# A new order of tasks and loads for a spectral filter and an MLP that share one core

## The chip, the core and the metric

The kernel runs on one core of a Trainium2 chip. The core has five engines that work at the same time and wait for each other through semaphores: TensorE (PE in the profile) for matmuls, VectorE (DVE), ScalarE (ACT), GpSimd (POOL) and SyncE (SP), which here only issues DMA transfers. TensorE writes its results to PSUM, which has eight banks; VectorE and ScalarE move them from there to SBUF. The metric is the device time of one execution in microseconds.

## The reference

Two independent branches are computed and mixed by a gate.

```python
def _A_ref(x, w_r, w_i):                      # x: 1 x 2048 x 512
    X = rfft2(x.astype(float32))
    X = X * (w_r + 1j * w_i)                  # W: 2048 x 257
    return irfft2(X, s=(S, D)).astype(bfloat16)

def _B_ref(x, w1, b1, w2):                    # w1: 512 x 1792, w2: 1792 x 512
    h = einsum("bsd,df->bsf", x, w1) + b1
    act = h * tanh(softplus(h))               # mish
    return einsum("bsf,fd->bsd", act, w2)

g = sigmoid((x * gate_w).sum(-1, keepdims=True))
return g * _A_ref(...) + (1 - g) * _B_ref(...)
```

## The kernel before

The dense branch is made of large matmuls that wait for little. It works on four chunks c of 512 rows. For a chunk, `mm1_c_ft` (line 795) is the product with one of 14 column tiles of w1 and takes four matmuls of 128x512; ScalarE evicts it with `mish_c_ft` (L811). Then `mm2_t_part` (L830) is the product with w2 for the row tile t = 4c to 4c+3, in two halves of seven matmuls (for the last tile, t = 15, in three column pieces instead). `bev_t` scales its result by 1 - g on its way to SBUF (L776 on ScalarE, L777 on VectorE).

The spectral branch is a long chain of small steps. Both transforms are split so that their halves are matmuls with constant matrices:

1. x is loaded (`ld_x`). Tiles 0 to 7 are transposed on TensorE (`tr`, L481). Tiles 8 to 15 are transposed in 32x32 blocks on VectorE (`tp`, L489), and 16 transfers from SBUF to SBUF, the shuffles (`sh`, named `xT<-act` in the profile), put the blocks in place; eight of them are issued by SP, eight by GpSimd.
2. Sums and differences (`ts`, `td`), then the transform along D: `a1` (L533), evictions `eg` on ScalarE and `e1p`, `e1m` on VectorE into `Abuf`.
3. The first half of the transform along S: `s1_t` for t = 0, 2, ..., 14 (L559), evictions `e2_t` into `Ybuf`.
4. The first exchange: each `e2_t` is followed by two writes to DRAM, `r1wta` and `r1wtb` (`scr<-Ybuf`); when all 16 have landed, four reads `r1r0` to `r1r3` bring the data back with partitions and columns rearranged (`Abuf<-scr`).
5. The filter stage, for u = 0 to 7 in pairs v: `s2_u` (L656); two multiplies with the weights W on VectorE, `wmu0`, `wmu1` (L414, `Qb<-ps,WT`); two sums on GpSimd, `wzu0`, `wzu1` (L414, `Zb<-Qb`); side steps for the two real-valued frequencies (`cv`, `crv`, `rcc`, `cm`, `chs`, `wc`); and `s2i_v` (L716), evicted by `e4_v0`, `e4_v1`.
6. The second exchange: four writes `r2w`, then four reads `r2r` (again `scr<-Ybuf` and `Abuf<-scr`).
7. For each row tile t: `s1i_t` (L744), eviction `e5_t` (L409 or L410), `a1i_t` (L755), `gc_t` on ScalarE (L760, scaled by g), `sam_t`, `sap_t` on VectorE (L766), `sbm_t`, `sbp_t`, nearly all on GpSimd (L414, `Tg<-Qb`). `sum_t` on VectorE adds this to the dense part (L414, `xo<-xo,Tg`), and each second one is followed by the store of two tiles. For tiles 14 and 15 `fin_t` (L842) does dense scaling and adding in one.

The weights W come in 18 pieces: `ld_Wp`, `ld_Wm` (eight each, about 128 KB) and two small `ld_Wz`. The names end in the part (0 real, 1 imaginary) and the group (0 to 3). All of them must be there before the first multiply. Further loads on SP are `ld_w2_0`, `ld_w2_1` and the constants `ld_rf`, `ld_ri`. The gate needs 16 `gdot` on VectorE (L575) and one power on GpSimd (`gpow`).

The program builds the list of all 639 tasks with what each reads and writes. It doesn't decide their order: that is written out beforehand in the string `ORDER`. `schedule` reads it from left to right. An entry is a task number of two base-62 digits; where a task may run on several engines a letter follows that says on which; where it takes a PSUM tile a digit follows with its first bank. From the order and the banks `schedule` derives the waits: a task waits for what it reads, and a task that takes a bank waits for those that still evict from it. Each engine, SP as well, works through its own part of the list strictly in order, so a task that waits holds all behind it on its engine. At the front TensorE runs 18 matmuls on constants (`warm`, L430).

Of the kernel before, what the change touches and what calls it, by code (L numbers as in the profile page):

```python
# [165 lines left out]
class _Graph:  # L166
# [89 lines left out]
DIGITS = "0123456789ABCDEFGHIJKLMNOPQRSTUVWXYZabcdefghijklmnopqrstuvwxyz"  # L256
ENGINE = {"p": "pe", "a": "act", "v": "dve", "g": "pool", "s": "sp"}
ORDER = (
    "0M04005060P070208090A000B0Q0C010R0D0E0F0G0H0T0I0x60J0N0yv0K0z50L7510V0O7F211610v13312v7K47A714v767L0S7M770U787"
    "B0W7C1Zv7G1X0037H1av1l50X1b61n1m33J0Y1Y0Z1pv7D7P00a17518v1d1B791A7T67U15116v1C191E7R51c60b1F1G7I7Q1D7N1Q7f01N1"  # L260
    "vv7J7h11V7b21ov1ev1wv7O1U1S7V41W7g7c8307E7S8J21fv1J1M8977i1P8H534283332718K1O1T1L36841y20v1x01gv0g0j1K7W381z0i"
    "8L41I0l8D68701R8M7z4297x18820v2Bv1H2Av8A21v350c2Iv2Ca2Hv7X02Jv8E22a7d32fv2D60s807y0f7Y0p2iv2gv7e2Kv1h10o2L41qv"
    "8l02N1iv0k2M32Ea1k8B48510e2Pv0u2V22W60q8n70m2hv8C2F2Ov8m2X861j0h2Yv2Zv1r30n1sa2Qa8b02312k62j32G8F42av8I24v262t"
    "52l1u2u38o2b12v2mv2nv1t2xv8177v52ca2R125822d2wv2ya2z68G372oa2e8p32Sv7w2p4392qv3A7Z130a8t68r22U3C8N73E8Z47a318u"
    "8h52T3B8q8a2r8c3G8x33D3F2s320d8j13H3I0r3K3L0t8k3T7s68f48O3O7t3W3P03M3N3Q8s8i3U3X18g3R8Pa3hv3S3Y47j77p07ua3a7q3"
    "gv3lv8d63kv3jg8y3Z3b7k8e7rv3t23ig3u43ng43v3V3v4F07la7m63mg8z74H903w42v47v3x46v7n3c79P24Ov4G37oa44g3y63d9X50w45"
    "g49g3e9Q4I4Sv9Y8v23z8w4J8Q748g4Pv4Tv4K28R4L403f3o3p34b08Sv8T23rv4M419T74A3qa9U8U4B34N4d4Rg8Va3s4kv4Qg4lv4Da4c0"
    "4Vg4W9V74Ca4e4Ug4mg4pv4f9W4E8W24ov4ng4g44h4i9N34qg4X49F04j4Za9114Yv9O4rg4s4t4924uv4va4a9Z49D38X9459G9J64w9L79E"
    "9M9709a8Ya93a954x5915H35Aa5P751496v5Qa9b29K5R55S4y9c5v15f75n65Iv5J352v5U5K5B4985T5wa4z5325C5M5L5oa5D5Wg5Vg5E5x"
    "55Ng5gv5y605Og9R15z5p350545X699a9H45Ya6R75q5Fg566J65Gg5h09S6Ka556Sv62gA1v5r9d56B16T29e61g5s5i9A76x66L36U5k6Ca6"  # L270
    "V6D55ug5Z15j6309I6EA8v58g57g5a5tgA2v6M5mg6p46W9B9yv5lg6N6Yg6ya6qa6h26ia6O9f66z2A7v5c6G5b706Xg5dg64aA5v719i45eg"
    "650A36Z36Pg6F6r59l1669Ca6Ig6j79zv6s9g6Qg6aa6b39j9m729p267689s0AEv6k6HgA4v6Ag74v6u6c6t9v5A96l69g6mA06wvA6ABv6d9"
    "ka6eAAv6vv6ogAC9haADv6ng9nAHv6fg73g6ggAF9o9qAGv9rAI9t9w9u9x"
)
NBF = 14
SHQ = ("pool", "sp", "pool", "sp")
# [688 lines left out]
```

## Time and profile before

| | us |
|---|---|
| median of three runs | 131.43 |
| lowest and highest of them | 130.37 and 131.91 |
| profiled execution | 131.48 |
| span of the profiled execution, first to last instruction | 129.7 |

The trace covers the span; the 1.8 us between span and time lie around it. A row of the order of time gives start and length in us, the engine, the line and the operation, the tiles out<-in and how many instructions are merged; in brackets stands how long the engine was idle before and what ended that. A row of the chain of waits gives start, length and the engine, tile and line. A row of a table by stretches gives the stretch, its length, the busy time of the engine asked for with the number of its instructions, the granted TensorE clock, the DMA share and GB/s. The clock was 1.00 throughout.

### The profile page before, as it was taken

Reading aid. Unit: us, or ns where it says so; the run is one execution under the profiler, and the core shown is the slowest. Engines: PE = TensorE matmul, PEld = TensorE weight load, DVE = VectorE, ACT = ScalarE, POOL = GpSimd, SP = SyncE. Lnnn points to the kernel's source line nnn. Section 1 sums busy time; section 2 is a strip of 40 time slices with the busy share of each in tenths; the row PEclk is TensorE's granted clock in tenths of the full one; section 3 lists DMA queues with packets and bytes.
Section 4 is the critical chain, followed back from the end, with each engine's and each line's share of the span. In section 5 each row is a group of like instructions: output and inputs, shape, how many; then the busy total and the mean of one; then the engine's idle time right before and its main releaser. Section 6 shows DMA issues by size and latency. Waiting matters only on the chain.

```text
span 129.7 us, 2726 instructions
## 1 busy us (share of the span) xinstructions
PE 123.0 (95%) x1014; PEld 66.1 (51%) x1014; DVE 91.6 (71%) x178; ACT 69.4 (54%) x119; POOL 56.3 (43%) x90
## 2 busy tenths in 40 slices
PE   7999999999999999699999999999999999999960
PEld 5776546445554444344444444444447666555650
DVE  0456999898699981179499795541006997999992
ACT  1306777798997537500336047454077988674300
POOL 4000047000000009146879499930000799979770
PEclk9999999999999999999999999999999999999999
DMA  3999618799998667991000032555089000224045
GB/s 88 337 402 394 199 40 219 216 263 189 289 314 242 197 173 223 331 390 43 0 5 3 0 93 73 162 162 159 13 285 356 3 5 3 81 81 157 10 152 172
DMA packets 19293, 21.16 MB, mean 163 GB/s; under 512 B 1744, under 2 KB 15952, under 8 KB 19152
## 3 DMA queue, kind: packets, MB, share of 16 engines
q1 hardware_dynamic: 18176, 19.67, 48.6%
q10 hardware_dynamic: 816, 0.79, 1.9%
q0 software_dynamic: 288, 0.53, 1.5%
q8 instruction: 8, 0.13, 0.4%
q14 instruction: 5, 0.04, 0.1%
HBM read 13.64 MB, written 6.29 MB: 154 GB/s over the span
## 4 chain that ended last, share of the span: by engine, by line
PE 85%; DMA 5%; DVE 3%; POOL 2%; issue 1%; POOLq 1%; DVEq 0%
PE ps L795 37%; PE ps L830 29%; DMA Abuf<-scr 5%; PE ps L744 3%; PE ps L755 3%; PE ps L533 3%; PE ps L559 3%; PE ps L430 3%; POOL Tg L414 2%; PE ps L656 2%; PE ps L716 2%; DVE Qb L766 1%; PE ps L481 1%; DVE xo L842 1%; DVE xT L409 1%
## 5 line engine op out<-in xcount | busy, mean ns | idle before, releaser
L795 PE MATMUL ps<-xT,w_sb 128*128 128x512 bf16 (+1 forms) x240 | 53.8, 365 | 0.3 <-DVE xT L409 0.3
L830 PE MATMUL ps<-w_sb,act 128*128 128x512 bf16 (+2 forms) x252 | 52.2, 355 | 0.0
L811 ACT ACTIVATE act<-ps,b1f 128x512 bf16<-128x512 f32 x56 | 36.5, 687 | 26.6 <-PE ps L795 26.6
L830 PEld LDWEIGHTS ps<-w_sb,act 128*128 128x128 bf16 x252 | 22.8, 98 | 23.0 <-issue 0.6
L795 PEld LDWEIGHTS ps<-xT,w_sb 128*128 128x128 bf16 x240 | 22.3, 98 | 21.9 <-DVE xT L409 0.8
L414 POOL TENSOR_TENSOR Tg<-Qb 128x256 bf16<-128x256 f32 x29 | 22.6, 812 | 17.4 <-DVE Qb L766 17.4
L414 POOL TENSOR_TENSOR Zb<-Qb 128x510 bf16<-128x510 f32 x16 | 20.0, 1268 | 3.2 <-DVE Qb L414 2.6
L414 DVE TENSOR_TENSOR Qb<-ps,WT 128x1024 f32<-128x1024 f32 x16 | 18.9, 1215 | 3.4 <-PE ps L656 3.3
L766 DVE SCALAR_TENSOR_TENSOR Qb<-ps,gcol,Qb 128x256 f32<-128x256 f32 x32 | 13.6, 473 | 1.5 <-issue 0.8
L580 POOL TENSOR_TENSOR gcol<-omg,gdot 128x16 f32<-128x16 f32 x1 | 2.9, 2942 | 26.6 <-DVE Tg L575 26.6
L410 ACT ACTIVATE Ybuf<-ps 128x1024 bf16<-128x1024 f32 x9 | 9.1, 1024 | 6.5 <-PE ps L716 6.2
L414 DVE TENSOR_TENSOR Abuf<-ps,Tg 128x512 bf16<-128x512 f32 x16 | 10.4, 685 | 2.7 <-ACT Tg L540 1.5
L409 DVE CAST Ybuf<-ps 128x1024 bf16<-128x1024 f32 x7 | 8.6, 1223 | 3.8 <-PE ps L716 3.1
L379 POOL DMA_DIRECT2D xT<-act x8 | 4.0, 503 | 15.5 <-DVE act L489 15.5
L575 DVE SCALAR_TENSOR_TENSOR Tg<-xo,Tg 128x512 bf16<-128x512 bf16 x16 | 10.5, 685 | 0.2
L776 ACT ACTIVATE xo<-ps,omg 128x512 bf16<-128x512 f32 x11 | 7.3, 687 | 5.2 <-PE ps L830 3.5
L777 DVE TENSOR_SCALAR xo<-ps,omg 128x512 bf16<-128x512 f32 x3 | 2.3, 751 | 10.8 <-PE ps L830 10.8
L760 ACT ACTIVATE Qb<-ps,gcol 128x256 f32<-128x256 f32 x16 | 7.1, 473 | 4.3 <-PE ps L755 4.2
L414 DVE TENSOR_TENSOR xo<-xo,Tg 128x512 bf16<-128x512 bf16 x14 | 9.0, 653 | 0.0
L540 ACT ACTIVATE Tg<-ps 128x512 f32<-128x512 f32 x8 | 4.7, 594 | 6.2 <-PE ps L533 6.2
L410 ACT ACTIVATE Zb<-ps 128x512 bf16<-128x512 f32 x12 | 7.0, 603 | 1.0 <-PE ps L744 1.0
L409 DVE COPY xT<-ps 128x512 bf16<-128x512 bf16 (+1 forms) x6 | 2.9, 505 | 5.7 <-PE ps L481 5.7
(61 smaller groups left out, 88.1 us busy)
## 6 DMA issues: line engine op xcount, KB each, us to landing
Abuf<-scr SPq DMA_DIRECT2D x8, 512.0 KB, 6.8
scr<-Ybuf SPq DMA_DIRECT2D x16, 128.0 KB, 2.2
scr<-Ybuf SPq DMA_DIRECT2D x4, 512.0 KB, 2.9
w_sb<-in_B_w_dram SPq DMA_DIRECT2D x2, 896.0 KB, 6.6
out_dram<-xo SPq DMA_DIRECT2D x7, 256.0 KB, 2.0
xo<-in_A_x_dram SPq DMA_DIRECT2D x3, 512.0 KB, 7.5
rt<-c_rt SPq DMA_DIRECT2D x2, 512.0 KB, 7.4
WT<-in_A_w_r_dram SPq DMA_DIRECT2D x7, 128.5 KB, 5.6
```

Source lines behind the costliest of these rows:

```text
L379: t = G.add(name, queue, issue if issue != 0.62 or queue != "pool" else 1.0, lambda e: e.dma_start(dst, src), reads=reads, writes=writes, ...
L409: fs = {"dve": ("dve", dve_dur(n, rate=rate), lambda e: e.tensor_copy(out=dst(), in_=src())), "act": ("act", act_dur(n), lambda e: e.activ ...
L410: "act": ("act", act_dur(n), lambda e: e.activation(dst(), src(), AF.Copy))}
L414: f = lambda e: e.tensor_tensor(out=o(), in0=i0(), in1=i1(), op=op)
L540: G.add(f"eg_{t}", "act", act_dur(512), lambda e, gb=gb, pa=pas[0], pv=pv: e.activation(G0[:, gb].rearrange("p t c (m s) -> p t c m s", s= ...
L575: lambda e, t=t: e.scalar_tensor_tensor(out=junk[t % 2], in0=xo[:, t, :], scalar=1.0, in1=gwb, op0=ALU.mult, op1=ALU.mult, accum_out=gdot[ ...
L760: lambda e, t=t, sl=sl, p5=p5: e.activation(gC[:, sl, :].rearrange("p (i n) -> p i n", i=2), ps[:, p5.bank, :].rearrange("p (i n) -> p i n ...
L766: lambda e, t=t, sl=sl, p5=p5, o=o, op=op: e.scalar_tensor_tensor(out=st1[:, sl, o::2, :], in0=ps[:, p5.bank, :].rearrange("p (i n) -> p i ...
L776: G.add_multi(f"bev_{t}", [("act", act_dur(512, True), lambda e: e.activation(xo[:, t, :], ps[:, pd.bank, :], AF.Copy, scale=omg[:, t:t + ...
L795: ins = e.matmul(o if c < 2 else o.rearrange("p (a t j) -> p a t j", a=4, t=4), w1_sb[:, i, 128 * ft:128 * (ft + 1)], xTp[:, i, 512 * c + ...
L811: lambda e, c=c, ft=ft, pd=pd, hb=hb: e.activation(act[:, hb, ft, :].rearrange("p (t a j) -> p t a j", t=4, a=4), ps[:, pd.bank, :].rearra ...
L830: ins = e.matmul(ps[:, pd.bank, cs_], act[:, hb, ft, 128 * tl:128 * (tl + 1)], w2_sb[:, ft, cs_], start=(ft == 0), stop=(ft == NFT - 1))
```

## The change

Only the string `ORDER` changes; the first and last lines of the diff stand for its 20 lines, which are all new:

```diff
 ORDER = (
-    "0M04005060P070208090A000B0Q0C010R0D0E0F0G0H0T0I0x60J0N0yv0K0z50L7510V0O7F211610v13312v7K47A714v767L0S7M770U787"
+    "0M04000050N060107080P090A0B0C0U0D0E0F0G0H0O0I0Q0x40J0K0yv0z110v0L7A20S750113135027F67K77612v7G14v0R1av77037B0T"
...
-    "ka6eAAv6vv6ogAC9haADv6ng9nAHv6fg73g6ggAF9o9qAGv9rAI9t9w9u9x"
+    "a6ngADv6d71AHv6wg7274vA36fg6ggAEv73gAF9nAGv9q9oAI9r9t9u9w9x"
 )
```

The tasks, their code and what they depend on are the same. What differs, decoded with the task list:

**SP.** The first 12 issues are the same, up to `ld_Wp00`. Then, up to `r1r0`:

```
before: sh12 sh32 sh31 sh33 sh11 sh13 sh30 sh10 w2_1 Wm02 Wz0 Wm03 Wm10 Wm00 Wz1 Wp02 Wm12 Wp12 Wp10
        r1w0b Wm01 w2_0 Wp13 Wp11 r1w6a r1w0a Wp03 Wm11 r1w6b r1w4b r1w2b r1w2a r1w4a r1w10a r1w10b
        r1w8b r1w14a r1w8a r1w12a r1w12b r1w14b Wp01 Wm13 rf r1r0
after:  Wm00 Wp01 Wm01 sh12 sh31 sh11 sh13 sh30 sh33 sh10 sh32 Wm12 Wp11 Wm13 w2_0 Wm11 r1w2a Wp03
        r1w2b Wp13 Wz1 Wp12 r1w4b Wm02 r1w0a r1w0b w2_1 Wp02 r1w6b Wz0 Wm03 r1w6a r1w8a r1w8b r1w4a
        r1w10b r1w10a r1w12a r1w12b r1w14b r1w14a Wp10 Wm10 rf r1r0
```

From there to the last `r2r` nothing changes; the stores at the end have another order.

**TensorE.** The first matmuls keep their kinds and change places. `s1` runs in the order 2, 0, 4, 6, 8, 10, 12, 14 (before 6, 0, 2, 4, 10, 8, 14, 12). Around the filter stage (`2_13` stands for `mm1_2_13`, `M2_0` for a half of `mm2_2`):

```
before: rcw s2_0 s2_1 M0_0 M2_0 M2_1 2_2 M0_1 s2_2 s2_3 s2_4 M1_0 2_13 M1_1 rcc_0 3_6 s2_5 rcc_1 3_10 2_11
        M5_0 rcc_2 M5_1 s2i_0 s2_6 M6_0 3_8 M6_1 s2i_1 s2_7 3_9 M7_0 rcc_3 3_5 s2i_2 3_1 M8_0 s2i_3 M8_1 3_11
        3_0 M7_1 M9_0 3_3 3_4 M10_0 M9_1 s1i_1 s1i_2 s1i_3 s1i_0 3_12 a1i_3 ...
after:  rcw 2_3 M1_0 s2_0 s2_1 2_6 M4_0 M4_1 s2_2 s2_3 M1_1 M5_0 rcc_0 s2_4 s2_5 M6_0 M6_1 rcc_2 M5_1 rcc_1
        s2i_0 2_8 M3_0 s2_7 s2_6 2_4 2_7 M3_1 rcc_3 s2i_1 M9_0 M9_1 s2i_2 3_9 M7_0 s2i_3 3_8 3_10 M7_1 M11_0
        3_2 M8_0 3_6 3_5 M8_1 M10_0 s1i_1 s1i_0 s1i_3 s1i_2 M11_1 a1i_0 ...
```

Ahead of `s2_0` stand 39 `mm1` and 4 halves of `mm2` before, 38 and 5 after. The last on TensorE before: `a1i_14 mm2_14_0 a1i_13 mm2_12_1 a1i_12 mm2_13_1 mm2_14_1 mm2_15_0 mm2_15_1 mm2_15_2`. After: `a1i_14 mm2_12_0 mm2_14_0 a1i_15 mm2_12_1 mm2_14_1 mm2_15_0 mm2_15_1 mm2_15_2`.

**VectorE, ScalarE and GpSimd** follow the new order. Of the `e2`, those for t = 0, 4, 8, 12 stay on VectorE and the others on ScalarE. Behind the first `sa`, VectorE has three `e5`, one `bev` and two `sb` (before two, none and three); GpSimd has 30 `sb` (before 29). VectorE's last tasks:

```
before: sam_14 sap_14 sap_13 sam_13 sbp_14 sum_9 sap_12 sam_12 sum_8 sbm_14 sum_10 fin_14_1 sum_13 fin_15_0 sum_12
        fin_15_1 fin_15_2
after:  sam_14 sum_7 sap_14 sam_12 sbm_14 sum_10 sap_12 sap_15 sum_13 sam_15 sbp_15 sum_11 fin_14_1 sum_12 fin_15_0
        fin_15_1 fin_15_2
```

GpSimd's last tasks: before `sbp_13 sbm_13 sbm_12 sbm_15 sbp_12`, after `sbm_13 sbp_14 sbm_12 sbp_12 sbm_15`.

More of the change, by code (lines that the diff above doesn't have):

```diff
@@ L258 @@
 ORDER = (
-    "0M04005060P070208090A000B0Q0C010R0D0E0F0G0H0T0I0x60J0N0yv0K0z50L7510V0O7F211610v13312v7K47A714v767L0S7M770U787"
[L260 to L272, printed above, removed]
-    "ka6eAAv6vv6ogAC9haADv6ng9nAHv6fg73g6ggAF9o9qAGv9rAI9t9w9u9x"
+    "0M04000050N060107080P090A0B0C0U0D0E0F0G0H0O0I0Q0x40J0K0yv0z110v0L7A20S750113135027F67K77612v7G14v0R1av77037B0T"
@@ new lines @@
+    "787L0V1X47C1Zv7M0W1l37H7N1Y0X1m17P51n1547R37Q1751ov1pv7O1b17I16v7D1A1B1d0Y7V40Z7T718v1C8L18357S190a7U1c30b7J3J"
+    "1F7X61E1G7b78M7W8H11D7E1wv1I331vv1fv7Y1ev1qa8J42720c1Q0d0e1N791R348B61J1U1K1M1O1S8I357c1r01H848C28737291x31T1W"
+    "1ga1P1y57z68521z2Bv1sa7h321v1L1h02Av20v87722v1iv1V8K867d42Jv2Kv2hv2307i7Z32Hv2V22Iv802L57e0p24v7a7x40m2gv0r2Ca"
+    "7f60u2iv2X880n2N1t2W32D07g0h2M72fv7v22Zv2Ea1u2Pv0q0s0o2Ov2Qa2Yv367w8x52u67y262R00g8y2j72t22k31j2Sv1k8d42l2nv2v"
+    "0v0f2mv2G8r70j2aa2xv2wv8e2oa0i2F2b18s2ca2ya8F52p32qv388G8t08u2T2z6392U258z18j030a8953A7p42e8Z28b32d908D63B3D3C"
@@ new lines @@
+    "8A3F7j72r3E2s8v13G8c8k3I7k7q8153H32318a0k0l3K3O3P38f20t3L3M3Q7m03R823N8E3T7lv8g3X53Y23Z8w8l73S3hv8N13gv3W3kv3U"
+    "7ra3a3jg8O3t48m3ig3u63lv3b42v7n43v3w8Q23c33V3v7oa3mg4F43d3ng8Pa4G045g47v4H8T34I46v44g3x4J8U8Va3e4K60w8R4Ov3f4P"
+    "v3y749g8Sa4L3o3z3p38p748g3qa4Qg4Sv4Tv7s24c04e3ra8q4b34kv8h54Rg4d8i4Vg4M8n68o404N414A7t4f4lv4g74h4ov4B34Dv4W947"
+    "4Ug4i4ng4j954mg4pv3s4Ca96a4X34s4rg4Zv4Ya9V04qg8W14t34vv9T79W9X04E4a8X4ua9A39H49154w9P67ua9Y9N04x929729O59093v5"
+    "155Av9U9I5P75H45Qa52v8Yv9B9Cv5305B75R15Ia545C4y5f49J5565J35ga5D5v4985S9Q5K555wa58g5h05n64z5X45E5i5Gg505T6B75L5"
@@ L274 @@
+    "U5ov5Ya9R15Z65p46Ca9K5M9D799v5Fg5k9S5q57g5a5j6D35Ng6325Wg64a9b06J55Og5x19yv9E5c5b9d25y9Z66h79c5lg5Vg9zv9e6505s"
+    "9F25r6E5z6ia6R75dg9a9L46Kv5mg6p56G6F9G5egA1v666Z69MA06aa605ug6j35tg6L2A5v686x1A4v6M9i46b66Hg676Sa6T06Ig6k69g6q"
+    "a6c9j62g6OA7v9ka6r76N6U9f56yvA2v9l26z16m9g9m9p4ABv6Ag61g6s6l9s3AAv6Qg6Pg6V6og6WAC9v06uA8v6Yg6tA970A66e6vv6Xg9h"
+    "a6ngADv6d71AHv6wg7274vA36fg6ggAEv73gAF9nAGv9q9oAI9r9t9u9w9x"
 )
```

## The prediction

> **What bounds the kernel now.** I read the page's busy times first, then the chain of waits, then TensorE's order of time, then the queues of SP, GpSimd and VectorE at the places that the chain names.
>
> ```profile
> span 129.7 us, 2726 instructions
> PE 123.0 (95%) x1014; PEld 66.1 (51%) x1014; DVE 91.6 (71%) x178; ACT 69.4 (54%) x119; POOL 56.3 (43%) x90
> ```
>
> TensorE works 123.0 of 129.7 us. No task is added or removed, so that sum stays. Only three things can move: TensorE's idle time, what follows its last matmul, and how early the long transform gets through beside the dense work.
>
> ```profile
> 6.86 1.91 PE L795 MATMUL ps<-xT,w_sb 128*128 128x256 bf16 x16 [0.27 <-DVE xT L409]
> 55.31 0.63 PE L656 MATMUL ps<-Abuf,rt 64*32 64x256 bf16 x32 [1.23 <-DMA Abuf<-scr]
> 119.10 6.28 PE L830 MATMUL ps<-w_sb,act 128*128 128x512 bf16 x56
> ...
> 119.32 1.66 DVE Qb L766 x4
> 121.05 1.71 POOL Tg L414 x2
> 123.87 0.88 POOL Tg L414
> 124.95 0.72 DVE xo L842
> 126.75 0.52 DVE xo L842 x2
> ```
>
> The first three rows are TensorE's, in order of time; the bracket is the idle time before and what ended it. Its one large hole is 1.23 us, in front of the first filter matmul s2_0 (L656): it waits for the first exchange through DRAM (r1r0) to land. The last matmuls end at 119.10 + 6.28 = 125.38. The other rows are the end of the chain: it leaves TensorE at 119.3, goes through VectorE (the sa tasks, L766) and GpSimd (the sb tasks), and VectorE's last fin (L842) ends at 126.75 + 0.52 = 127.27, which is 1.9 after the last matmul. The remaining 129.7 - 127.27 = 2.4 us are the last store. So the end is set by VectorE and GpSimd, and those started late:
>
> ```profile
> 100.40:127.30 26.90, 25.89 (x55) 1.00 0.18 66
> 101.38 2.10 POOL L414 TENSOR_TENSOR Tg<-Qb 128x256 bf16<-128x256 f32 x3 [15.84 <-DVE Qb L766]
> ```
>
> The first row is VectorE alone from the first sa to the last fin: 25.89 busy of 26.90, 1.0 idle. GpSimd sat 15.84 us idle before its first sb. Whatever brings the first s1i (L744) forward moves this whole tail.
>
> **First exchange: SP's queue.** SP issues one transfer after the other, and each waits in that order.
>
> ```profile
> 7.26 0.58 SPq L379 DMA_DIRECT2D WT<-in_A_w_r_dram  x1
> 17.57 5.02 SPq L379 DMA_DIRECT2D xT<-act  x8
> 37.32 8.53 SPq L379 DMA_DIRECT2D scr<-Ybuf  x13
> 48.40 2.43 SPq L379 DMA_DIRECT2D Abuf<-scr  x4
> ...
> 48.40 6.87 DMA Abuf<-scr
> ...
> 26.56 2.43 DVE L414 TENSOR_TENSOR Tg<-xT 128x512 bf16<-128x512 bf16 x7
> ```
>
> After the first W piece (7.26) SP stands still until the last transpose lets the shuffles go (17.57). From there to r1r0 at 48.40 it issues 45 transfers almost without a pause, 8.53/13 = 0.656 us each. So r1r0 is late because SP is, not because its data are: the last s1 is over long before. The change puts three more W pieces into the dead time before 17.57, which leaves 42 issues: 3 x 0.656 = 2.0 us. r1r0 goes at 46.4 and, with the same 6.87 (the row of the chain), lands at 53.3. The three pieces can delay the shuffles behind them by what they still have to move; I take nothing. SP issued its last shuffle before 17.57 + 5.02 = 22.6, and VectorE reads shuffled data first at 26.56 (last row): what the 4 us leave after the landing is the cover, and each us beyond it would hold VectorE's evictions of the first stage. The early r1w2, r1w4 wait for their evictions in the same queue and would hold the W pieces behind them; TensorE now does s1_2 and s1_4 8 to 12 us earlier than before, so I cost that at nothing, with 1.4 us of cover (next paragraph).
>
> **TensorE up to s2_0.** The prices, from the chain (a dense up matmul group mm1, half a down group mm2, one s2i, four s1i):
>
> ```profile
> 60.58 0.86 PE ps L795 x4
> 61.45 1.51 PE ps L830 x7
> 86.13 0.57 PE ps L716 x32
> 97.82 0.89 PE ps L744 x16
> ```
>
> Counting the decoded queue, s2_0 has 38 mm1 and 5 half mm2 in front of it, before 39 and 4: +1.51 - 0.86 = +0.65. Its turn comes at 55.31 - 1.23 + 0.65 = 54.7. r1r0 lands at 53.3, so the hole goes, with 1.4 us to spare. If SP gained nothing the landing would be at 55.27 and the wait 0.6. The 0.27 at 6.86 stays: the tasks up to there have only changed places.
>
> **Filter stage and second exchange.** From s2_0 to the last s2i_3 the old queue took 86.13 - 55.31 = 30.8 us, with 9 mm1 and 12 half mm2 between; the new one has 5 and 12: 30.8 - 4 x 0.86 = 27.4, so s2i_3 comes at 82.1 instead of 86.1. From s2_0 to the first s1i there are 10 mm1 instead of 13 (17 halves in both): 97.65 - 55.31 - 2.6 = 39.7, so s1i_1's turn is at 94.4. The second exchange must fit:
>
> ```profile
> 93.08 1.76 SPq L379 DMA_DIRECT2D Abuf<-scr  x4
> DMA to landing us min/median/max: 4.0/5.4/6.7
> ```
>
> Before, its first read was issued at 93.08 and landed 4.0 later, 97.1, which is 11.0 after s2i_3. From 82.1 that is 93.1, 1.3 us ahead of s1i_1's turn. What is late next is GpSimd:
>
> ```profile
> 57.00:86.00 29.00, 22.77 (x32) 1.00 0.18 61
> 58.31 1.26 POOL L414 TENSOR_TENSOR Zb<-Qb 128x510 bf16<-128x510 f32 x1 [1.64 <-DVE Qb L414]
> 85.31 0.23 POOL L703 TENSOR_TENSOR Zb<-ch 128x8 bf16<-128x8 f32 x1
> L414 DVE TENSOR_TENSOR Qb<-ps,WT 128x1024 f32<-128x1024 f32 x16 | 18.9, 1215 | 3.4 <-PE ps L656 3.3
> 62.89 0.85 PE L656 MATMUL ps<-Abuf,rt 64*32 64x256 bf16 x48
> ```
>
> Its 32 filter tasks (wz and their small helpers) are 22.77 us of work, in order. Before they ran from 58.31 (3.0 after s2_0) to 85.54, so 4.5 idle. Now they start at 57.7, could end at 80.5, and s2i_3 wants them by 82.1: at most 1.6 us idle are allowed. I take it that this holds, because the idle time came from TensorE's order: the old queue gave the second pair, s2_2, at 62.89, 7.6 us after s2_0, and VectorE's 16 multiplies stood 3.3 us for such matmuls. The new one puts one mm1 and two halves between the pairs (0.86 + 3.02), so s2_2 comes at some 59.2, before the four multiplies of the first pair are over (54.7 + 0.5 + 4 x 18.9/16 = 59.9).
>
> **The tail.** s1i_1 at 94.4; then four s1i (0.89) and one half mm2 (1.51) and a1i_0 (0.22 and the drain of its last matmul) with its scaled eviction on ScalarE (0.47), some 1.0 together: the first sa starts at 97.8, before at 100.4. VectorE's list behind it is that of before with one more eviction and one more bev, and one sb less:
>
> ```profile
> L414 DVE TENSOR_TENSOR xo<-xo,Tg 128x512 bf16<-128x512 bf16 x14 | 9.0, 653 | 0.0
> L414 DVE TENSOR_TENSOR Tg<-Qb 128x256 bf16<-128x256 f32 x3 | 2.3, 765 | 0.0
> L409 DVE CAST Zb<-ps 128x512 bf16<-128x512 f32 x2 | 1.4, 686 | 0.1
> L760 ACT ACTIVATE Qb<-ps,gcol 128x256 f32<-128x256 f32 x16 | 7.1, 473 | 4.3 <-PE ps L755 4.2
> ...
> 99.57 0.22 PE ps L755 x4
> ...
> 97.86 0.75 DVE L777 TENSOR_SCALAR xo<-ps,omg 128x512 bf16<-128x512 f32 x1 [9.85 <-PE ps L830]
> ```
>
> 0.69 + 0.75 - 0.77 = +0.7, so 26.6 of work; with the old 1.0 idle the last fin ends at 97.8 + 26.6 + 1.0 = 125.4, and with 2.4 for the last store the span is 127.8. TensorE does not stand in the way: its last matmul is at 125.38 - 1.23 = 124.15. Nor does GpSimd: 30 sb of 22.6/29 = 0.78 from some 99 end at 122.4 to 123.5.
>
> ```profile
> L414 POOL TENSOR_TENSOR Tg<-Qb 128x256 bf16<-128x256 f32 x29 | 22.6, 812 | 17.4 <-DVE Qb L766 17.4
> ```
>
> The profiled execution took 131.48, 1.8 more than its span, and the median of the runs is 131.43, so both are one number here: 127.8 + 1.8 = **129.6**, 1.4% under before. Without idle time on VectorE the last matmul sets the end: 124.15, a fin of 0.5, the store 2.4, and 1.8: 128.8.
>
> **Rivals.** *The filter stage does not shrink.* If GpSimd idles its old 4.5 us there, s2i_3 waits until 57.7 + 22.77 + 4.5 = 85.0, 2.9 late, TensorE stands with nothing to put in (its queue is in order), and s1i and the tail go with it: 132.5. For it: GpSimd now has almost no slack, and each late multiply costs TensorE in full beyond 1.6 us. Against it: the pauses of before are named as waits for matmuls that now come sooner. Half of it gives 131.
>
> *Slower: the sums meet the adds.*
>
> ```profile
> 124.08 0.95 DVE L414 TENSOR_TENSOR xo<-xo,Tg 128x512 bf16<-128x512 bf16 x1
> 125.61 0.41 DVE L414 TENSOR_TENSOR xo<-xo,Tg 128x512 bf16<-128x512 bf16 x1
> 123.84 1.77 POOL L414 TENSOR_TENSOR Tg<-Qb 128x256 bf16<-128x256 f32 x2
> 101.00:126.00 25.00, 22.63 (x29) 1.00 0.15 56
> ```
>
> The same sum takes 0.95 beside GpSimd's last two adds (123.84 + 1.77 = 125.61) and 0.41 after them. The 14 have a mean of 0.65. If all 14 were long, VectorE would need 14 x 0.30 = 4.2 more, the end would go to 133.8; from 4 more long ones (2.2) the gain is gone, from 6 it is slower than before by 1%. For it: GpSimd now runs from 99 to 123 with hardly a pause, so most sums run beside it. Against it: before, GpSimd was busy 22.63 of 25.0 us while the sums ran (last row), hardly less, and their mean was 0.65. The Trainium skill has this as a rule (SBUF — State Buffer, Who interferes with whom): a VectorE instruction with both inputs in SBUF contends with a GpSimd one that reads SBUF, and the later one blocks until the other is done. By that rule the difference 0.95 - 0.41 is the rest of a GpSimd add, and the trace agrees, since an add is 0.81 and the loss 0.54. Read strictly, every sum that meets an add is long, which is this rival.
>
> *Bank turns.* The new queue often takes PSUM banks with little to spare: s2_4 reuses the banks of s2_2 when six multiplies are over, 54.7 + 0.5 + 6 x 18.9/16 = 62.3, and its turn (one mm1, four halves and some 1.1 of small matmuls after s2_0) is 62.7. Several such turns lost by 0.2 to 0.4 each give 1.5 to 2 us, 131.3. For it: their number; against it: the old queue, laid out as densely, lost nothing but the DMA wait.
>
> That the change does not do what it says (no earlier W) would need SP to be blocked at the pieces; they wait for nothing. Even then it costs the 0.6 above, 130.2.
>
> **Numbers.** A change of 1% (130.1 and 132.7) is about what a measurement of this kernel can tell from none: the three runs of before lie between 130.37 and 131.91. Chances: forecast 0.56, filter stage 0.20, sums 0.12, bank turns 0.12. Faster takes 0.52 of the forecast and 0.03 of the bank turns; same the rest of these, 0.12 of the filter stage and 0.04 of the sums; slower 0.08 and 0.08: 0.55, 0.29, 0.16. The range begins at 128.4, a little under the bound without idle time since each eviction on VectorE may overlap, and reaches to 132.4, which takes in the bank turns and nearly all of the filter case.
>
> **What would show it.** SP: three more W pieces before 17.6, r1r0 issued at 44 to 46.5. TensorE: s2_0 at about 54.8 with no DMA wait; s2i_3 near 82; first s1i near 94.5. GpSimd: idle under 1.6 us in the filter stage. VectorE: first sa near 98, last fin near 125.4, mean sum near 0.65. A TensorE wait on GpSimd (L716) shows the first rival, a mean sum over 0.8 the second, many short waits on banks the third. r1r0 landing after 55, or s1i waiting for its DMA, would prove the two exchange steps wrong.

## The result, and the profile after

| | before | after |
|---|---|---|
| median, us | 130.91 (4 runs) | 129.50 (4 runs) |
| lowest and highest, us | 130.37 and 131.91 | 129.17 and 129.98 |
| profiled execution, us | 131.48 | 129.98 |
| its span, us | 129.7 | 128.2 |

The measured ratio of the two is 0.988, with a 95% interval of 0.983 to 0.993: 1.2% faster (the two medians alone give 0.989). (The string `ORDER` has 15 lines, not 20 as the section on the change says.)

The order of time of the changed kernel, TensorE's rows at the places that the prediction named:

```profile
7.19 1.47 PE L795 MATMUL ps<-xT,w_sb 128*128 128x256 bf16 x12 [0.73 <-DMA w_sb<-in_B_w_dram]
...
55.28 0.63 PE L656 MATMUL ps<-Abuf,rt 64*32 64x256 bf16 x32
...
82.50 0.64 PE L716 MATMUL ps<-Zb,rt 32*64 32x256 bf16 x32
...
94.95 1.06 PE L744 MATMUL ps<-GMs,Abuf 128*128 128x128 bf16 x16
...
118.07 6.28 PE L830 MATMUL ps<-w_sb,act 128*128 128x512 bf16 x55
```

The row of s2_0 (55.28) has no bracket any more: the wait of 1.23 us for the first exchange is gone. s2i_3 comes at 82.50 (86.06 before), the first s1i at 94.95 (97.65). The last matmuls end at 118.07 + 6.28 = 124.35, 1.03 earlier than before, though 1.23 of waiting went: at 7.19 TensorE now waits 0.73 for a piece of w1, where it had waited 0.27 for VectorE.

SP in the same view:

```profile
7.43 2.58 SPq L379 DMA_DIRECT2D WT<-in_A_w_r_dram  x4
18.89 5.03 SPq L379 DMA_DIRECT2D xT<-act  x8
...
47.53 2.07 SPq L379 DMA_DIRECT2D Abuf<-scr  x4
```

Four pieces of W now stand in front of the shuffles. But the shuffles go out at 18.89, 1.3 later than before, and r1r0 at 47.53 instead of the 46.4 of the prediction.

The tail, by the end of the chain of waits (first fence), by the busy time of VectorE and then of GpSimd in stretches (second and third), and by groups of instructions (fourth; columns: busy time, mean ns of one, idle time before). A q behind an engine's name, as in DVEq and SPq, marks its sequencer, which waits and issues:

```profile
119.58 4.00 PE ps L830 x35
123.61 0.74 DVE xo L842
124.34 0.33 DVE xo L414
124.67 0.40 DVEq L900
125.07 0.52 DVE xo L842 x2
```

```profile
98.30:125.60 27.30, 26.04 (x57) 1.00 0.17 63
```

```profile
98.30:125.60 27.30, 23.31 (x30) 1.00 0.17 63
57.00:82.10 25.10, 22.67 (x32) 1.00 0.17 55
```

```profile
L414 POOL TENSOR_TENSOR Tg<-Qb 128x256 bf16<-128x256 f32 x30 | 23.3, 812 | 18.1 <-DVE Qb L766 18.1
L414 DVE TENSOR_TENSOR Qb<-ps,WT 128x1024 f32<-128x1024 f32 x16 | 18.8, 1213 | 0.1
L414 DVE TENSOR_TENSOR xo<-xo,Tg 128x512 bf16<-128x512 bf16 x14 | 8.8, 630 | 0.0
```

The last fin ends at 125.07 + 0.52 = 125.59, before at 127.27. The chain passes from TensorE to VectorE at 123.61, but that is not a wait for TensorE: the task there, fin_14_1, needs the matmuls of mm2_14_1, which were over at some 121.1, where the narrower ones of mm2_15 begin, and VectorE was busy with a sum until it began. The 14 sums have a mean of 0.630 (0.653 before). In the filter stage GpSimd's 22.67 of work lie between 58.27 (its first sum there) and 82.00, so it was idle 1.1 us, where it had been idle 4.5; and the multiplies wait 0.1 in all, where they had waited 3.4.

### The profile page after: what moved, and what is told of

It reads as the page before. It is cut to its first block, busy times and chain, and to the rows that moved or that the text cites. A ratio compares the mean times of both kernels' runs of the same rounds, so it can differ in the third digit from the quotient of the medians.

```text
span 128.2 us, 2717 instructions
## 1 busy us (share of the span) xinstructions
PE 121.6 (95%) x998; PEld 65.8 (51%) x1014; DVE 91.9 (72%) x178; ACT 67.1 (52%) x118; POOL 56.9 (44%) x91
## 4 chain that ended last, share of the span: by engine, by line
PE 80%; DMA 8%; DVE 4%; SPq 4%; issue 1%; DVEq 0%
PE ps L830 37%; PE ps L795 29%; DMA xo<-in_A_x_dram 8%; SPq L379 4%; PE ps L744 3%; PE ps L755 3%; PE ps L559 3%; PE ps L533 2%; PE ps L716 2%; DVE act L489 2%; PE ps L656 2%; DVE xo L842 1%; DVE Tg L414 1%; DVE Tg L575 0%; DVEq L900 0%
## 5 line engine op out<-in xcount | busy, mean ns | idle before, releaser
L830 PE MATMUL ps<-w_sb,act 128*128 128x512 bf16 (+2 forms) x240 | 50.3, 354 | 0.7 <-issue 0.2
L811 ACT ACTIVATE act<-ps,b1f 128x512 bf16<-128x512 f32 x56 | 36.0, 690 | 22.5 <-PE ps L795 17.2
L414 POOL TENSOR_TENSOR Tg<-Qb 128x256 bf16<-128x256 f32 x30 | 23.3, 812 | 18.1 <-DVE Qb L766 18.1
L776 ACT ACTIVATE xo<-ps,omg 128x512 bf16<-128x512 f32 x9 | 6.1, 688 | 13.7 <-PE ps L830 7.8
L414 DVE TENSOR_TENSOR Abuf<-ps,Tg 128x512 bf16<-128x512 f32 x16 | 10.1, 683 | 1.6 <-PE ps L533 1.6
L410 ACT ACTIVATE Ybuf<-ps 128x1024 bf16<-128x1024 f32 x9 | 9.1, 1022 | 2.9 <-PE ps L716 2.9
L777 DVE TENSOR_SCALAR xo<-ps,omg 128x512 bf16<-128x512 f32 x5 | 3.7, 747 | 9.5 <-PE ps L830 9.4
L410 ACT ACTIVATE Zb<-ps 128x512 bf16<-128x512 f32 x11 | 6.4, 603 | 1.8 <-PE ps L744 1.8
```

The source lines that it names most:

```text
L410: "act": ("act", act_dur(n), lambda e: e.activation(dst(), src(), AF.Copy))}
L414: f = lambda e: e.tensor_tensor(out=o(), in0=i0(), in1=i1(), op=op)
L776: G.add_multi(f"bev_{t}", [("act", act_dur(512, True), lambda e: e.activation(xo[:, t, :], ps[:, pd.bank, :], AF.Copy, scale=omg[:, t:t + ...
L811: lambda e, c=c, ft=ft, pd=pd, hb=hb: e.activation(act[:, hb, ft, :].rearrange("p (t a j) -> p t a j", t=4, a=4), ps[:, pd.bank, :].rearra ...
L830: ins = e.matmul(ps[:, pd.bank, cs_], act[:, hb, ft, 128 * tl:128 * (tl + 1)], w2_sb[:, ft, cs_], start=(ft == 0), stop=(ft == NFT - 1))
```

## The experiments

Each was timed against the kernel before on the same chip; ratios are to that, with a 95% interval. The key times of the profiled executions, in us from the start of the span:

| kernel | SP's first shuffle | r1r0 issued, landed | s2_0 | s2i_3 | first s1i | first sa | last matmul ends | last fin ends | span |
|---|---|---|---|---|---|---|---|---|---|
| before | 17.57 | 48.40, 55.27 | 55.31 | 86.06 | 97.65 | 100.42 | 125.38 | 127.27 | 129.7 |
| after, first profile | 18.89 | 47.53, 54.07 | 55.28 | 82.50 | 94.95 | 98.37 | 124.35 | 125.59 | 128.2 |
| after_again | 17.32 | 45.33, 52.07 | 54.50 | 81.72 | 94.17 | 97.59 | 123.57 | 124.81 | 127.4 |
| pieces_back | 17.47 | 48.12, 54.46 | 54.66 | 81.87 | 94.33 | 97.74 | 123.72 | 124.96 | 127.6 |
| pieces_after_x | 17.32 | 45.81, 52.72 | 54.55 | 81.77 | 94.22 | 97.64 | 123.62 | 124.85 | 127.5 |
| old_pieces_front | 17.80 | 46.98, 53.04 | 54.29 | 85.04 | 96.63 | 99.40 | 124.36 | 126.26 | 128.7 |
| a1i_late | 17.57 | 45.57, 51.77 | 54.95 | 82.17 | 94.62 | 99.55 | 125.02 | 126.27 | 128.9 |
| a1i_later | 17.68 | 46.01, 53.17 | 55.06 | 82.28 | 94.73 | 100.52 | 126.00 | 127.24 | 129.9 |
| e5_15_act | 17.91 | 46.34, 52.60 | 55.00 | 82.21 | 94.67 | 98.09 | 124.06 | 125.31 | 127.9 |

### Which part of the change brings the gain

**pieces_back**: the changed kernel, with the three early pieces put behind the shuffles again.

```diff
 SP:
-ld_Wp00 ld_Wm00 ld_Wp01 ld_Wm01 sh12 sh31 sh11 sh13 sh30 sh33 sh10 sh32 ld_Wm12
+ld_Wp00 sh12 sh31 sh11 sh13 sh30 sh33 sh10 sh32 ld_Wm00 ld_Wp01 ld_Wm01 ld_Wm12
```

> The changed kernel with its three added W pieces issued behind SP's shuffles again; all engines keep the new order. Theory (the gain comes from the new order on TensorE; the early pieces only keep the first exchange ahead of TensorE's turn): x12 lands near 15.0 instead of 16.35, the shuffles start near 17.6 instead of 18.9, the three issues come back behind them (2.0 us), so the first exchange read goes out near 48.2 instead of 47.5 and lands near 54.8; TensorE's turn for s2_0 stays near 55.2 and the time within 0.3 us of the changed kernel (129.5). Rival (the early pieces are the gain): the time goes back to that of the kernel before, 130.9, with a DMA wait of about 1 us in front of s2_0.

Measured: 129.70 us, ratio 0.987 (0.980 to 0.994). Its order of time, SP and TensorE:

```profile
48.12 2.08 SPq L379 DMA_DIRECT2D Abuf<-scr  x4
...
54.66 0.63 PE L656 MATMUL ps<-Abuf,rt 64*32 64x256 bf16 x32
```

r1r0 goes out as late as in the old kernel, lands at 54.46, and s2_0 starts at 54.66 without a wait. The early pieces buy margin (2.4 us in after_again, 0.2 here) and no measurable time in the new order. The margin of 0.2 is that of one execution: from issue to landing r1r0 took 5.9 to 7.2 us in the profiles of this study, here 6.34. By these it could land up to 0.7 behind s2_0's turn in other executions without the early pieces (an estimate). The gain is in the rest of `ORDER`.

**old_pieces_front**: the kernel before, with the same three pieces in front.

```diff
 SP:
-ld_Wp00 sh12 sh32 sh31 ...
+ld_Wp00 ld_Wm00 ld_Wp01 ld_Wm01 sh12 sh32 sh31 ...
```

> The kernel before with only the three W pieces moved in front of the shuffles. Theory: the first exchange read goes out some 0.7 to 0.9 us earlier than its 48.4 (2.0 us of issues saved, 1.3 lost because x12 lands later), the hole of 1.23 in front of s2_0 shrinks to about 0.4, and the time falls by some 0.8 at most, to 130.1 or above. Rival (the early pieces are the gain): the whole 1.4 us, 129.5.

Measured: 130.81 us, ratio 0.995 (0.991 to 0.999). Its order of time:

```profile
46.98 2.07 SPq L379 DMA_DIRECT2D Abuf<-scr  x4
...
54.29 0.63 PE L656 MATMUL ps<-Abuf,rt 64*32 64x256 bf16 x32
```

The hole in front of s2_0 goes here too, and everything behind it comes about 1.0 us earlier than before. So in the old order the pieces are worth 0.5%. In the new order no gain shows, since in pieces_back s2_0's turn came only when r1r0 had landed anyway.

**pieces_after_x**: the first profile had the shuffles 1.3 us late, because x12 (the last piece of x) had landed at 16.35 instead of 15.03. An interim theory held that the three pieces, in flight with x, had delayed it. Here the pieces wait on SP until x has landed.

```diff
-nbytes=256 * 514, bw=190e3, nd=16, issue=0.45)
+nbytes=256 * 514, bw=190e3, nd=16, issue=0.45, deps=[G.last_w[("x", 12)]] if (i, g) == (0, 1) else [])
```

(and the same for `ld_Wm00` and `ld_Wm01`)

> The changed kernel with its three early W pieces held on SP until x12 has landed; nothing else. Theory (the pieces in flight slow x12's landing): x12 lands near 15.0 again, the pieces still go out before the last transpose is over, the shuffles start near 17.6, the first exchange read goes out near 46.2 and lands near 52.8, over 2 us ahead of TensorE's turn; the time stays within 0.3 us, since nothing waits for that exchange. Rival 1 (x12's later landing is chance or comes from elsewhere): x12 stays at 16.3. Rival 2 (the end hangs on the first exchange): the time falls by about 1.3 us.

Measured: 129.29 us, ratio 0.983 (0.977 to 0.989).

**after_again**: the changed kernel once more, unchanged.

> The changed kernel once more, unchanged, for a second profile and a time beside the others of this set. Theory (the 16.35 us at which x12 landed in its first profile was chance, since two other kernels with the same pieces in flight had it at 14.3 and 14.9): x12 lands at 14.3 to 15.1, the first exchange read goes out near 45.6 and s2_0 starts near 54.6. Rival (the pieces in flight delay x12): x12 lands after 16 again. Time 129.3 to 129.7 in both.

Measured: 129.66 us, ratio 0.988 (0.984 to 0.991). SP in the order of time up to 20 us, pieces_after_x first and after_again second:

```profile
7.70 9.04 SPq L379 DMA_DIRECT2D WT<-in_A_w_r_dram  x4
17.32 3.10 SPq L379 DMA_DIRECT2D xT<-act  x5
```

```profile
7.53 2.58 SPq L379 DMA_DIRECT2D WT<-in_A_w_r_dram  x4
17.32 3.11 SPq L379 DMA_DIRECT2D xT<-act  x5
```

In the one the last piece is issued only after x is there (7.70 + 9.04 = 16.74), in the other all four by 10.1, and the shuffles go at 17.32 in both. x12 landed at 14.78 in both. So the interim theory fell: the pieces do not delay x, and the 16.35 of the first profile was that execution's own. It was also the slowest of its four runs (129.98; lowest 129.17). The ratio of pieces_after_x is lower than that of after_again, but the intervals overlap and none of its key times in the table is earlier, so no gain is claimed for it.

### What lateness costs behind the filter stage

**a1i_late** and **a1i_later**: dense work put back in front of the tail, so that the same tasks start it later. What ran as a1i_late moves only `mm2_10_1` (1.5 us), not both tasks that its expectation names; a1i_later moves both (1.51 + 0.86 = 2.4 us).

```diff
 TensorE, a1i_late:
-mm2_11_1 a1i_0 a1i_1 a1i_3 s1i_5 mm1_3_3 a1i_2 s1i_7 mm2_10_1
+mm2_11_1 mm2_10_1 a1i_0 a1i_1 a1i_3 s1i_5 mm1_3_3 a1i_2 s1i_7
 TensorE, a1i_later:
+mm2_11_1 mm2_10_1 mm1_3_3 a1i_0 a1i_1 a1i_3 s1i_5 a1i_2 s1i_7
```

> The changed kernel with 2.4 us of dense work (mm2_10_1 and mm1_3_3) moved from behind the first a1i tasks to in front of a1i_0; the sum of TensorE's work is the same. Theory (VectorE's list behind its first sa sets the end): the first sa comes 2.4 us later, near 100.8; of the 1.2 us that VectorE idles in that list most goes, so its last fin ends 1.2 to 2.0 later and the time is 130.7 to 131.5. Rival (TensorE's end sets the time): TensorE's last matmul stays at 124.4 and the time within 0.3 us of 129.5.

> The changed kernel with both mm2_10_1 and mm1_3_3 in front of a1i_0 (2.4 us of dense work moved; in the run a1i_late only mm2_10_1, 1.5 us, had been moved, and that gave 130.6). Theory (VectorE's list behind its first sa sets the end): the first sa another 0.9 later, near 100.4, and the time 131.1 to 131.6. Rival (TensorE's own waits set it): the time stays at 130.6.

Measured: a1i_late 130.59 us, ratio 0.994 (0.990 to 0.997); a1i_later 131.22 us, ratio 1.000 (0.998 to 1.002). VectorE's first sa in the order of time of a1i_later:

```profile
100.52 1.26 DVE L766 SCALAR_TENSOR_TENSOR Qb<-ps,gcol,Qb 128x256 f32<-128x256 f32 x3 [2.43 <-ACT Qb L760]
```

First sa 100.52, in the old kernel 100.42; last fin 127.24, in the old one 127.27; time the same. Everything else of the change is still in this kernel (no hole, filter stage 3.4 us shorter), and none of it counts when the tail starts at its old time. Whatever the change gains, it gains by starting the tail earlier. TensorE's end moved as well, to 126.00, though its work is the same: two of its `s1i` now wait 1.0 us in all for ScalarE's evictions `e5` (L410). So this run alone doesn't tell VectorE's end from TensorE's; small_adds, below, does.

**wz_twice**: the prediction's first rival, as a price. wz60 and wz70 on GpSimd are computed twice, the extra copy into dead space.

```diff
+                if twice is not None:
+                    e.tensor_tensor(out=Tg[:, 1024 * twice:1024 * twice + 510]..., in0=i0(), in1=i1(), op=op)
                 return e.tensor_tensor(out=o(), in0=i0(), in1=i1(), op=op)
```

> The changed kernel with the first sum of each of the last two filter steps (wz60 and wz70 on GpSimd) computed twice, the extra copy into dead space: 2 x 1.26 = 2.5 us more work for GpSimd in the filter stage, nothing else changed. The theory (the prediction's first rival, as a price): GpSimd's last sum ended at 82.00 in the changed kernel, 0.4 us or less ahead of s2i_3, so all but that shows: GpSimd ends 2.5 later, TensorE gets a hole of some 2.1 us in front of s2i_3 with GpSimd named as the releaser, the first s1i, the first sa and the last fin come 2.1 later each, and the whole gain is gone: 131.2 to 131.9, ratio to before 1.00 (0.997 to 1.006). Rival: the stage has slack that the order of time does not show, since the second exchange and the dense matmuls behind s2i_3 make the delay good: hole under 1 us, first s1i and end less than 1 us later, ratio 0.987 to 0.993.

Measured: 131.18 us, ratio 0.999 (0.996 to 1.002). Its order of time, TensorE and GpSimd (L416 is the extra copy):

```profile
83.61 0.64 PE L720 MATMUL ps<-Zb,rt 32*64 32x256 bf16 x32 [1.70 <-POOL Zb L417]
...
81.08 1.26 POOL L416 TENSOR_TENSOR Tg<-Qb 128x510 bf16<-128x510 f32 x1
82.30 1.25 POOL L417 TENSOR_TENSOR Zb<-Qb 128x510 bf16<-128x510 f32 x1
```

Of 2.5 us more on GpSimd 1.70 stand as a hole on TensorE, with GpSimd as its releaser, and the ratio rises by 0.011 against after_again, 1.5 us: the whole gain. The expectation had 2.1. Measured from s2_0, GpSimd's last filter task ended 2.2 later than in after_again, as 0.3 of the copies fell into its short waits; and 0.5 of that was slack, not 0.4.

### What sets the end

**e5_15_act**: one eviction, e5_15, goes from VectorE to ScalarE, to see whether VectorE's list alone sets the end.

```diff
 VectorE:
-sap_10 e5_15 sum_3
+sap_10 sum_3
 ScalarE:
+e5_15
```

> The changed kernel with the eviction e5_15 on ScalarE instead of VectorE, ahead of bev_13 where ScalarE idles for 1.3 us. Theory (VectorE sets the end, TensorE's last matmul lies 0.8 us lower): VectorE's list is 0.6 us shorter, its last fin ends 0.5 to 0.6 earlier with TensorE's end unchanged, the time falls by 0.4 to 0.6, to 128.9 to 129.1. Rival (TensorE or the stores set the end): no change, 129.3 to 129.7.

Measured: 129.59 us, ratio 0.988 (0.984 to 0.992): nothing gained. **pieces_after_x_e5_act**, the same with the pieces waiting for x:

> Both small changes together: the three early W pieces held until x12 has landed, and e5_15 on ScalarE. Theory: holding the pieces is worth 0 to 0.2, the eviction 0.4 to 0.6: 128.7 to 129.0. Rival (neither matters): 129.3 to 129.7.

Measured: 129.49 us, ratio 0.987 (0.984 to 0.990): nothing either. VectorE in e5_15_act, by stretches and in order of time:

```profile
98.00:125.35 27.35, 25.54 (x56) 1.00 0.17 63
```

```profile
115.66 0.88 DVE L766 SCALAR_TENSOR_TENSOR Qb<-ps,gcol,Qb 128x256 f32<-128x256 f32 x2 [0.20 <-ACT Qb L760]
116.86 0.48 DVE L766 SCALAR_TENSOR_TENSOR Qb<-ps,gcol,Qb 128x256 f32<-128x256 f32 x1 [0.33 <-POOL Tg L414]
```

From the first sa to the last fin it takes as long as in after_again (27.35 for a stretch with 26.07 busy there), with 0.53 less work: the saving became waits, 0.20 for ScalarE in the first row and 0.33 for GpSimd in the second. `sam_14`, the second row, writes into the slot of `st1` that GpSimd's adds of tile 10 still read (tiles share four slots), so VectorE can run ahead of GpSimd only by so much. The time is that of the rival, but its reason isn't shown by this: the last fin still ends 1.25 behind the last matmul.

**small_adds**: GpSimd's adds in the tail made small. Only 8 of 128 columns of the sb are computed, those of tiles 8 to 11 are a memset, and sbm_15 and VectorE's two stay whole, so most of the last combination is left out.

```diff
+                k = slice(0, 128 if (t, nm) in ((14, "m"), (15, "m"), (15, "p")) else 8)
+                if 8 <= t < 12:
+                    G.add_multi(f"sb{nm}_{t}", [("pool", 0.3, lambda e, o=o: e.memset(o, 0.0))], reads=[("st1", sl, 0), ("st1", sl, 1)], writes=[("ga", t, nm)])
+                    continue
-                tt(f"sb{nm}_{t}", lambda o=o: o, lambda sl=sl: st1[:, sl, 0:2, :], lambda sl=sl: st1[:, sl, 2:4, :], op, 256,
+                tt(f"sb{nm}_{t}", lambda o=o, k=k: o[:, :, k], lambda sl=sl, k=k: st1[:, sl, 0:2, k], lambda sl=sl, k=k: st1[:, sl, 2:4, k], op, 256,
```

> The changed kernel with GpSimd's adds in the tail made small: of the sb for tiles 0 to 7, 12 and 13, and of the ones of tile 14 and 15 that GpSimd has, only 8 of 128 columns are computed (sbm_15 and VectorE's two in full), and the eight for tiles 8 to 11 become a memset. So most of the last combination is left out; VectorE's and TensorE's lists stay. Theory (VectorE and GpSimd hold each other up in the tail, TensorE is 0.7 us ahead of them): the 14 sums go from a mean of 0.63 to 0.41-0.45 us, VectorE waits for no GpSimd add and has idle time before the last fins, the last fin ends 0.5 to 0.65 after the last matmul (1.24 now), and the time falls by 0.6 to 0.75 against the changed kernel: ratio to before 0.981 to 0.983. Rival (the long sums have another cause, such as TensorE's or ScalarE's traffic, and VectorE's list alone sets the end): the sums keep 0.6 or more, the last fin stays 1.1 to 1.25 behind the last matmul, ratio 0.987 to 0.988.

Measured: 127.78 us, ratio 0.974 (0.970 to 0.978), twice the gain of the change. Sums, then VectorE's last rows in order of time:

```profile
L414 DVE TENSOR_TENSOR xo<-xo,Tg 128x512 bf16<-128x512 bf16 x14 | 6.3, 452 | 0.0
```

```profile
120.24 0.95 DVE L414 TENSOR_TENSOR xo<-xo,Tg 128x512 bf16<-128x512 bf16 x1
...
123.01 0.35 DVE L846 SCALAR_TENSOR_TENSOR xo<-ps,omg,Tg 128x128 bf16<-128x128 f32 x1 [0.30 <-PE ps L834]
123.79 0.35 DVE L846 SCALAR_TENSOR_TENSOR xo<-ps,omg,Tg 128x128 bf16<-128x128 f32 x1 [0.43 <-PE ps L834]
```

Thirteen sums take 0.41 or 0.42; the one long sum (0.95) is the one beside the whole add sbm_15. The last fins now wait for TensorE, and the last ends at 124.14, 0.4 behind the last matmul (123.76). So GpSimd's adds cost the end 1.24 - 0.38 = 0.86 us by way of VectorE. The other part of the gain, 0.75, was not expected: from the last fin to the end of the span it is 1.9 us instead of 2.6. That led to the next kernel.

**two_store_queues**: in after_again SP issues the last stores like this (order of time; the first row merges all six of 122 to 127 us, the second the last two of them):

```profile
122.93 2.97 SPq L379 DMA_DIRECT2D out_dram<-xo  x6
...
124.97 0.94 SPq L379 DMA_DIRECT2D out_dram<-xo  x2
```

Six stores, the last five back to back, the last one issued at 125.46, 0.65 after its fin has ended. Here two of the six are issued by ScalarE, which has nothing left to do.

```diff
-nbytes=128 * 2048, is_out=True, prio=PR["fin"], tail=0.6)
+queue="act" if t == 13 else "sp", nbytes=128 * 2048, is_out=True, prio=PR["fin"], tail=0.6)
...
+queue="act" if (t, part) == (15, 1) else "sp", nbytes=256 * (cs_.stop - cs_.start), is_out=True, ...
```

> The changed kernel with two of its last six stores (the one of tiles 12 and 13, and the middle piece of tile 15) issued by ScalarE, whose last own work ends at 120.5; all else as in the changed kernel. Theory (the last stores queue on SP: in the changed kernel's profile SP issues the last five stores back to back, 0.49 apart, and the last one goes out at 126.24, 0.65 after its fin's end at 125.59): the last store goes out within 0.1 of the last fin's end, last fin to end of span falls from 2.62 to about 2.0, the time by 0.5 to 0.65, ratio to before 0.982 to 0.984. Rival (what follows the last fin is the transfer itself and its completion, SP's queue hides in it, since the stores share the same DMA engines): last fin to end stays at 2.4 or more, ratio 0.987 to 0.988.

Measured: 128.88 us (128.75 to 129.18), ratio 0.983 (0.981 to 0.985). Its order of time:

```profile
124.31 0.33 SPq L379 DMA_DIRECT2D out_dram<-xo  x1
124.57 0.34 ACTq L379 DMA_DIRECT2D out_dram<-xo  x1
124.83 0.33 SPq L379 DMA_DIRECT2D out_dram<-xo  x1
```

The last fin ends at 124.80, its store goes out at 124.83, and the span is 127.0 (127.4). From the last fin to the end it is 2.2 us; the expectation had 2.0. This is the shortest time of the study for a kernel with the reference's whole work, 1.7% under before and some 0.4% under the changed one. By the ratio pieces_after_x stands level, with a wider interval (0.977 to 0.989), and the intervals of this kernel and after_again (0.981 to 0.985 and 0.984 to 0.991) still overlap a little. So the gain is shown by the profile, where the span is 0.4 us shorter with the last fin unchanged, more than by the times.

**two_queues_sb10**: the same, with e5_15 on ScalarE and one of GpSimd's adds, sbm_10, on VectorE in its place.

```diff
 VectorE:
-sap_10 e5_15 sum_3
+sap_10 sbm_10 sum_3
```

> The kernel with two store queues, in which also e5_15 goes from VectorE to ScalarE and sbm_10 from GpSimd to VectorE, in e5_15's place. VectorE's own work stays nearly the same (0.67 less, 0.42 to 0.85 more), GpSimd has 29 adds instead of 30 (0.9 less). Theory (VectorE and GpSimd hold each other up in the tail, so one add less on GpSimd counts although VectorE does it): GpSimd's last add ends 0.6 to 0.9 earlier, more of VectorE's last sums run after it (0.41 instead of 0.95), the last fin ends 0.2 to 0.6 earlier against the last matmul (1.24 before), and the ratio is 0.002 to 0.005 under that of the kernel with two store queues alone. Rival (VectorE's list alone sets the end): the last fin comes 0 to 0.2 later, the ratio is the same or up to 0.002 higher.

Measured: 129.55 us, ratio 0.988 (0.986 to 0.990): 0.5% slower than without it. GpSimd in order of time, and the sums:

```profile
116.78 3.15 POOL L414 TENSOR_TENSOR Tg<-Qb 128x256 bf16<-128x256 f32 x4 [0.28 <-DVE Qb L766]
120.69 2.46 POOL L414 TENSOR_TENSOR Tg<-Qb 128x256 bf16<-128x256 f32 x3 [0.76 <-DVE Qb L766]
```

```profile
L414 DVE TENSOR_TENSOR xo<-xo,Tg 128x512 bf16<-128x512 bf16 x14 | 9.4, 671 | 0.0
```

Now GpSimd waits for VectorE and ends at 123.15 instead of 122.62. VectorE exchanged 0.67 of eviction for 0.44 of add, but its sums grew from 0.630 to 0.671, 14 x 0.041 = 0.6, so its list is 0.4 longer. The theory that a lighter GpSimd is always worth it fell. The rival had the right direction, since here VectorE's list sets the end, but it held that list as a fixed sum: the last fin came 0.5 later and not 0 to 0.2, because the same sums took longer in their new places (why is said in the next section).

## Why the prediction was right

**The sum.** Predicted 129.6, measured 129.50. The path from SP to the last fin went as it said, term by term. That the figures agree to 0.1 us is in part luck: the first sa came at 98.37 and 97.59 in the two profiles of this kernel (predicted 97.8), VectorE's stretch behind it was 0.4 too long in the forecast and the store 0.2 too short, and the 131.43 from which the forecast went down was 0.5 above the 130.91 of the kernel's four runs, so that the gain was put at 1.8 us and measured at 1.4.

**First exchange.** "r1r0 goes at 46.4 and lands at 53.3": in the first profile 47.53 and 54.07, in after_again and six further kernels that have early pieces, 45.2 to 47.0 and 51.8 to 53.2. The step is right; the first profile is off it by its own late x12. (By the lists SP issues 44 and 41 transfers ahead of r1r0; the 45 and 42 of the prediction count r1r0 itself. The difference of three, on which the sum rests, stays. s1_2 and s1_4 came 11.3 and 6.8 us earlier, not 8 to 12, and no cost of the early r1w2 and r1w4 shows in r1r0's time.) "I take nothing" for the shuffles' delay by the three pieces is shown by pieces_after_x. What the prediction did not see is that the new order had little use for this step: it reckoned with 0.6 of waiting if SP gained nothing. In pieces_back SP gained nothing and the wait was zero: r1r0's way took 6.34 instead of the assumed 6.87, and it landed at 54.46, just ahead of s2_0.

**TensorE's turn and the filter stage.** s2_0 was put at 54.7 (55.28; 54.50 in after_again), the stage at 27.4 us (27.22 in both), s2i_3 at 82.1 (82.50; 81.72). "At most 1.6 us idle are allowed" to GpSimd: it took 1.1. The second exchange was nearer than thought: its first read was put at 11.0 after s2i_3, 1.3 us ahead of s1i_1's turn, and landed 11.6 after it (94.13), 0.8 ahead. The first rival did not come, for the reason given: the multiplies waited 0.1 in place of 3.4. Its price was right as well, since wz_twice turned 1.70 us of GpSimd's lateness into 1.5 us of time. The first s1i was put at 94.4 (94.95; 94.17), the first sa at 97.8 (98.37; 97.59).

**The tail.** VectorE was to have 26.6 of work and 1.0 idle; it had 26.04 and 1.3. The work was over-sized because its two adds took 0.64 on average (0.85 and 0.44) and not 0.77, and the sums 0.630 and not 0.653. The last fin was put at 125.4 (125.59; 124.81), the last matmul at 124.15 (124.35; 123.57).

**"Nor does GpSimd" stand in the way** is the weak sentence. GpSimd ends when the prediction said (123.40, within 122.4 to 123.5), but it is in the way twice on the way there: by the slots of `st1` (e5_15_act) and by making VectorE's sums long (0.630 against 0.452 in small_adds, 2.5 us over the 14). The old profile held the long sums in VectorE's 25.89 us of work and its waits in the 1.0 idle, and as the change hardly touched them, the forecast did not suffer.

**"2.4 for the last store"** was carried over as one number (2.62 after). It has a queue in it: with SP relieved, 2.2.

**The sums' rival** did not happen: the mean fell. The Trainium skill's rule, that the later of a VectorE and a GpSimd instruction on the shared port blocks until the other is done (SBUF — State Buffer, Who interferes with whom), is borne out, but the rival read it wrongly. Two sums of after_again, each behind the add that was running when it began (order of time):

```profile
116.18 0.72 POOL L414 TENSOR_TENSOR Tg<-Qb 128x256 bf16<-128x256 f32 x1
116.75 0.43 DVE L414 TENSOR_TENSOR xo<-xo,Tg 128x512 bf16<-128x512 bf16 x1
...
121.71 0.91 POOL L414 TENSOR_TENSOR Tg<-Qb 128x256 bf16<-128x256 f32 x1
121.96 0.94 DVE L414 TENSOR_TENSOR xo<-xo,Tg 128x512 bf16<-128x512 bf16 x1
```

The adds end at 116.90 and 122.62, the sums at 117.18 and 122.90, both 0.28 later. Of the 13 sums that began during an add, 12 end 0.28 to 0.29 after that add; the other began 0.04 before its add's end and took 0.41, as long as a sum alone. The adds lose as well: those that began during a sum, or during one of VectorE's own two adds, took 0.90 to 0.99, the others 0.72 or 0.73. The other profiles in which the adds are whole show the same 0.28 to 0.29. So a sum that meets an add is not always long. It lasts as long as the rest of that add and 0.28 more, here from 0.41 to 0.94, and with GpSimd hardly busier than before the mean stayed near its old size. Where the sums fall decides it, and that is what two_queues_sb10 changed.

**Bank turns** were not lost either. The view of TensorE's waits in after_again (total, times, longest) has two rows, both of the first 7 us:

```profile
PE ps L430 <- PEq L950: 0.8, 1, 0.8
PE ps L795 <- DVE xT L409: 0.2, 1, 0.2
```

## What to carry to other kernels

When every engine works through a fixed list, look for the one place from which a chain of small steps can no longer be made up (here the first sa), and price each edit by what it does to that time: 2.4 us of other work put in front of it cost 1.3% of the time, and all else that the change improved was worth nothing without it. Removing a wait on the way there gives margin rather than time if the wait's turn has moved too. Price a sum on VectorE beside a stream of adds on GpSimd by the rest of the add that it meets, not by its time alone. At the very end, look at the queue that issues the stores: five in a row on one queue hold the last one back, and an idle engine can issue some of them.

## What was not expected of the hardware

The fourth write of the second exchange, r2w3, took longer to land than its three sisters in some kernels. The queue view of a stretch (82 to 92 us) of the changed kernel, then of pieces_back; the columns are packets, MB and share of 16 engines, or KB each and median us to landing:

```profile
q8 instruction: 1, 0.02, 1.1%
...
scr<-Ybuf SPq DMA_DIRECT2D x1, 512.0 KB, 5.0
```

```profile
q8 instruction: 1, 0.02, 0.6%
...
scr<-Ybuf SPq DMA_DIRECT2D x1, 512.0 KB, 2.9
```

In both a single packet of 16 KB, a load of instructions, falls into the stretch. By the packets of the trace it started at 85.61 in the first, 1.1 us after r2w3 had been issued (84.52), and took 1.72 us; r2w3 landed 5.04 after its issue. In pieces_back the load started at 83.47, before r2w3 was issued (83.90), and the write took 2.91. All fourteen profiles divide this way: 4.0 to 5.2 us in the ten where the load began 0.85 to 1.6 us after the write's issue, 2.9 to 3.1 in the four where it began 0.4 to 0.6 ahead of it. That is an observation from the times; no kernel was made to move the load, so the cause is not shown. It cost nothing here, since r2r0 landed at least 0.4 us ahead of the first s1i in each of them.
